# A decode step of attention and a gated unit: the output projection's weights in five loads instead of eight

## The chip, the cores and the metric

One core of a Trainium2 chip runs the whole kernel. The time is device microseconds (us) of one execution; lower is better. Before the change it is 684.75 us, the median of three runs (684.56 to 685.55).

## What is computed

One token of width 512 goes through a layer norm, then through attention with 32 heads over a cache of 8192 keys and values of width 128, all in float32, and through a gated unit. The two results are multiplied and added to the input.

```python
xn = _layernorm(x)
q = (xn @ wq).reshape(B, Sq, H, Dh).transpose(0, 2, 1, 3)
scores = jnp.einsum("bhqd,bhkd->bhqk", q, k_cache) * (Dh ** -0.5)
o = jnp.einsum("bhqk,bhkd->bhqd", softmax(scores), v_cache)
s = o.transpose(0, 2, 1, 3).reshape(B, Sq, H * Dh) @ wo
g = gated(xn, w_gate, w_up, w_down)
return x + s * g
```

Here `gated` stands for `_silu((sigmoid(xn @ w_gate) * (xn @ w_up)) @ w_down)`. The two caches hold 256 MB, `wq` and `wo` 8 MB each.

## The kernel before, in words

All large loads go through one queue, that of SyncE (SP), in an order written out by hand. `wq`, `w_gate` and `w_up` come first, then keys and values of two heads at a time (a pair; `NP` = 16 pairs), 8 MB of keys and 8 MB of values each, and last `wo`. Three buffers of 64 KB a partition, `slots`, hold them: keys alternate between slots 0 and 1, values use slot 2, and `wo` comes into slot 1 when the last keys there have been used (`summed[NP - 2]`). `load` (a DMA at line 168) and `load_values` (a DMA at line 227) issue them.

For each pair, VectorE multiplies the keys by the query and sums (`scores`, lines 415 and 416), ScalarE makes the powers (`powers_of`), and TensorE multiplies them with the values (`pair`): 32 products of 4 key positions each, in turn into four groups of 32 PSUM rows (the 32 columns of the array that write such a group are called a tile here). A float32 product runs as two passes in the profile. `taken` makes TensorE wait for a piece of values, and `halved` and `valued` tell SyncE that half or all of the slot may be loaded again. The values of the last two pairs come in pieces: `V_HALVES` is the halves of the 128 columns of blocks (`NB`), `V_THREE` cuts at 64 and 104.

All TensorE instructions are noted first (`Later`) and played at line 38, so line 38 is every TensorE instruction of the profile, and the pairs are a loop on that engine.

Behind the last pair the heads' results are turned and divided into `o_all` (`heads_out` and `place`, lines 423, 469 and 472). The projection by `wo` is 32 rows per partition (`WR`), of 2 KB each: row `r` of all partitions, 256 KB, times column `r` of `o_all`. Its loads end at the rows `W_ENDS`. Each row below `W_FOLD` = 28 is either TensorE's, one product of 512 columns into the tile that `W_PE` names, or VectorE's (`W_DVE`, lines 513 and 515), which adds into two sums, `part`, in turn. `landed` makes an engine wait at the first of its rows in a piece. Line 518 adds the two sums, `to_fold` (line 490) adds what TensorE has in `big[0]`, and `fold` sums over partitions, with four products of 128 columns. Rows 28 to 31 go directly into the result's form, `acc`, by four products of 128 columns each. In TensorE's order the fold stands behind row 30 and ahead of row 31. Lines 539 and 541 multiply by the gate and add the input, and line 565 stores.

Ahead of the `wo` rows TensorE makes two products into `po` whose result nobody reads; they wait for nothing ("idle products" here). SyncE waits for the last load but one of `wo` (`ld_o[-2]`, line 556) before it leaves the body.

Of the kernel before, what the change touches and what calls it, by code (L numbers as in the profile page):

```python
# [51 lines left out]
def kernel(  # L52
# [18 lines left out]
    NB = S // HP  # L71
    NP = H // 2
    NG = 4
# [14 lines left out]
    FC = FL // GP  # L88
    assert F <= 3 * QT and FL % GP == 0 and 2 * KT * F <= SLOT and (FP + FC) * D <= SLOT // 2

    W_ENDS, W_FOLD = (10, 18, 23, 26, 28, 30, 31, 32), 28
    W_PE = [(0, 0), (1, 0), (2, 0), (3, 0), (4, 0), (10, 1), (11, 1), (12, 1), (18, 2), (19, 2), (23, 2), (24, 3), (26, 2), (27, 3)]
    W_DVE = [r for r in range(W_FOLD) if r not in [r for r, _ in W_PE]]
    V_CUTS, K_CUTS = (NB // 2, NB * 13 // 16), {NP - 2: (NB * 3 // 4,), NP - 1: (NB // 2,)}

    N_SEMS = 38
    DVE, ACT, SP, POOL = nc.vector, nc.scalar, nc.sync, nc.gpsimd
    PE = Later(nc.tensor)
    pe_only = OrderedEngineSet([nc.tensor.engine])
# [2 lines left out]

    sems = [nc.alloc_semaphore(f"s_{i}") for i in range(N_SEMS)]
    s_out = nc.alloc_semaphore("s_out")
# [42 lines left out]
    def semaphore(name):  # L147
        return unused.pop(0)
# [25 lines left out]
    def wait(eng, *steps):  # L174
        for s in steps:
            if s is not None:
                eng.wait_ge(*s)


    turned, spread_m, valued, picked = (semaphore(f"s_{n}") for n in ("turned", "spread", "valued", "picked"))  # L180
    maxed, reduced, powers, copied = (semaphore(f"s_{n}") for n in ("maxed", "reduced", "powers", "copied"))
    added = semaphore("s_added")
    q_made, q_spread, q_free = (semaphore(f"s_{n}") for n in ("q_made", "q_spread", "q_free"))
    s_val = [semaphore(f"s_val{n}") for n in range(3)]
    halved = semaphore("s_halved")


# [14 lines left out]
    def rows_of(src, i):  # L202
        rows = src.rearrange("b h s d -> (b h s) d")[2 * i * S:2 * (i + 1) * S, :]
        return rows.rearrange("(p j) d -> p (j d)", p=P)
# [3 lines left out]
    def pieces(*ends):  # L208
        return [slice(a, b) for a, b in zip((0,) + ends, ends + (NB,))]

    FULL, V_HALVES, V_THREE = pieces(), pieces(V_CUTS[0]), pieces(*V_CUTS)

    def cols(j):
        return slice(j.start * Dh, j.stop * Dh)

    def load_keys(i, cut, *after):
        n = (i + 1) % 2
        wait(SP, *after)
        for j in cut:
            ld_k.setdefault(i, []).append((j, load(SP, f"k{n}_{j.start}", slots[n][:, cols(j)], rows_of(k_cache, i)[:, cols(j)])))  # L220

    def load_values(i, cut, *after):

        wait(SP, *after)
        for j in cut:
            sem = s_val[((0,) + V_CUTS).index(j.start)]
            SP.dma_start(slots[2][:, cols(j)], rows_of(v_cache, i)[:, cols(j)]).then_inc(sem, 16)  # L227

    load_keys(0, FULL)
# [10 lines left out]
    ld_xr = load(ACT, "xr", x_row[0:P:GP, :], xv.rearrange("(g c) -> g c", g=NG), c_xrow)  # L240
    ACT.nop().then_inc(q_free, NK)
    ACT.nop().then_inc(s_val[1], 16 * (NP - 2))
    ACT.nop().then_inc(s_val[2], 16 * (NP - 1))
    pool(POOL.memset(ones, 1.0))
    pool(POOL.memset(eps_t, EPS))
    pool(POOL.memset(zeros, 0.0))
# [35 lines left out]
    def taken(sem, n):  # L282
        PE.wait_ge(sem, n)
        PE.nop().then_inc(sem, -n)
# [72 lines left out]
    n = FL // NG  # L357
# [11 lines left out]
    wait(PE, act(ACT.copy(s_gate, big[0])))  # L369
    gated = column_sums(big[1], s_gate)  # L370
    load_values(0, FULL, gated)
    wait(ACT, gated)
    c_sig = act(ACT.activation(g_row, big[1][:, :GC], AF.Sigmoid))


    def pair(v):
        taken(maxed, 1)
        PE.matmul(pt[0:1, :], mx[:, 0:1], ident, start=True, stop=True).then_inc(turned, 1)
        taken(reduced, 1)
        PE.matmul(pm[:, :2], ones[:1, :], mx[:1, 1:3], start=True, stop=True).then_inc(spread_m, 1)  # L380
        taken(powers, 2)
        PE.matmul(pm[:GP, 2:], rs.to_broadcast([P, GP]), half, start=True, stop=True).then_inc(added, 1)

        for j in range(0, NB, HT):
            if j in (0,) + V_CUTS:
                if j == V_CUTS[0]:
                    ins.then_inc(halved, 1)
                taken(s_val[((0,) + V_CUTS).index(j)], 16)
            g = j // HT % NG
            ins = PE.matmul(po[g * GP:g * GP + 2 * HT, :], weights[:, j // HT, :], v[:, j * Dh:(j + HT) * Dh],  # L390
                            start=(j < HT * NG), stop=(j >= NB - HT * NG))
        ins.then_inc(valued, 1)
        taken(copied, 1)
        for b in range(HT):
            ins = PE.matmul(pn[:2, :], pick[:, b:2 * HT:HT], o1[:, b * Dh:(b + 1) * Dh],
                            start=(b == 0), stop=(b == HT - 1))
        ins.then_inc(picked, 1)

    before = PE.take()
    pair(slots[2])  # L400
    each = PE.take()

# [3 lines left out]
    def all_max(i):  # L406
        DVE.wait_ge(turned, i + 1)
        DVE.reduce_max(mx[:1, 1:3], pt[0:1, :].rearrange("o (e p) -> o e p", e=2), axis=AX.X).then_inc(reduced, 1)  # L408

    def scores(i):  # L410
        k = slots[(i + 1) % 2].rearrange("p (j d) -> p j d", d=Dh)
        for j, ld in ld_k[i]:
            wait(DVE, ld)
            n = j.stop - j.start
            wait(DVE, dve(DVE.tensor_mul(k[:, j, :], k[:, j, :], qb[:, i:i + 1, :].to_broadcast([P, n, Dh]))))  # L415
            summed[i] = dve(DVE.reduce_sum(sc[i % 2][:, j], k[:, j, :], axis=AX.X))  # L416
        wait(DVE, summed[i])
        DVE.reduce_max(mx[:, 0:1], sc[i % 2], axis=AX.X).then_inc(maxed, 1)

    def heads_out(i):  # L420
        DVE.wait_ge(picked, i + 1)
        o = o_t[:, 2 * WP * i:2 * WP * i + Dh].rearrange("r (e a) -> r a e", a=WP)
        turned_out[i] = dve(DVE.transpose(o, pn.rearrange("e (a r) -> e a r", r=WR)))  # L423


    def powers_of(i):
        ACT.wait_ge(spread_m, i + 1)
        wait(ACT, act(ACT.mul(nb, pm[:, :2], -SCALE)))  # L428
        for e, h in enumerate(HALF):
            ACT.activation(weights[h, :, e * HT:(e + 1) * HT], sc[i % 2][h].rearrange("p (g b) -> p g b", b=HT),  # L430
                           AF.Exp, bias=nb[h, e:e + 1], scale=SCALE, accum_out=rs[h]).then_inc(powers, 1)

    def parts(i):
        ACT.wait_ge(added, i + 1)
        t = act(ACT.copy(den[:GP, 2 * i:2 * i + 2], pm[:GP, 2:]))
        ACT.wait_ge(valued, i + 1)
        ACT.copy(o1, po).then_inc(copied, 1)  # L437
        return t

    for i in range(NP):  # L440
        if i > 0:
            all_max(i - 1)
        if i >= 2:
            load_keys(i, pieces(*K_CUTS.get(i, ())), summed[i - 2])
            if i < NP - 1:
                load_values(i - 1, FULL, (valued, i - 1))
        if i == NP - 1:
            for v, cut in ((i - 1, V_HALVES), (i, V_THREE)):
                load_values(v, cut[:1], (halved, v))
                load_values(v, cut[1:], (valued, v))  # L450
        scores(i)
        if i > 0:
            powers_of(i - 1)
            parts(i - 1)
            heads_out(i - 1)
        if i == 1:
            wait(DVE, c_sig)
            c_gate = dve(DVE.tensor_mul(g_row, g_row, big[1][:, :GC]))
# [43 lines left out]
    def landed(eng, r, rows):  # L502
        k = rows.index(r)
        wait(eng, piece[r] if k == 0 or piece[r] != piece[rows[k - 1]] else None)

    t_parts = [placed, None]
    for k, r in enumerate(W_DVE):
        n = k % 2
# [8 lines left out]
    wait(DVE, max(t_parts, key=lambda t: t[1]))  # L517
    t_part = dve(DVE.tensor_add(part[0], part[0], part[1]))

    for n in range(2):  # L520
        PE.matmul(po[:2 * HT, :], weights[:, 0, :], slots[2][:, n * QT:(n + 1) * QT], start=True, stop=True)
    wait(PE, placed)
    w_rows, w_tiles = zip(*W_PE)
    for k, (r, g) in enumerate(W_PE):
        landed(PE, r, w_rows)
# [76 lines left out]
```

## Time and profile before

| what | us |
|---|---|
| median of three runs | 684.75 |
| the profiled execution | 684.87 |
| its span in the profile | 683.5 |
| VectorE busy in it | 613.1 |
| TensorE busy in it (matmuls) | 222.8 |
| ScalarE busy in it | 44.5 |

The profile is one execution. Its span is from the first instruction to the last; the execution's own time is 1.37 longer. PE is TensorE's matmuls, PEld its weight loads, DVE VectorE, ACT ScalarE, SPq the queue of SyncE. Times in the rows further down are microseconds from the span's start. What is in brackets behind a row is how long the engine had been idle and what released it. "issue" there means that the profile shows nothing it waited for.

### The profile page before, as it was taken

The page shows a single profiled execution, that of the slowest core. Times are in us where ns is not written, and L with a number is a line of the kernel's source. Part 1 is how long each engine was busy: PE and PEld are TensorE (multiplying, and loading weights), DVE is VectorE, ACT ScalarE, POOL GpSimd, SP SyncE. Part 2 cuts the span into 40 slices and gives each one's busy share as a digit, 9 for nine tenths or more (in the row PEclk, how much of TensorE's full clock was granted, in tenths as well). Part 3 has the DMA queues.
Part 4 walks back from the last instruction along what each step waited for, and adds up shares of the span by engine and source line. Part 5 has one row for each costly group of instructions (what it writes and reads, how often), then busy time and mean ns, then how long its engine had stood idle before and what let it go on. Part 6 is the DMA issues. An engine that isn't in the chain of part 4 may idle for free. (4 is left out here: it accounts for less than half of the span.)

```text
span 683.5 us, 3414 instructions
## 1 busy us (share of the span) xinstructions
PE 222.8 (33%) x1386; PEld 63.6 (9%) x1386; DVE 613.1 (90%) x151; ACT 44.5 (7%) x142; POOL 2.6 (0%) x11
## 2 busy tenths in 40 slices
PE   0353024060513306050412406050422406060678
PEld 0120001010100101010100101010100101010111
DVE  3879999999999898998979899898979899999926
ACT  2130010000000100000000100000010100000010
POOL 0000000000000000000000000000000000000000
PEclk9996657575665757575665757575575757566789
DMA  9999999999999999999999999999999999999998
GB/s 386 429 436 468 433 430 430 430 430 430 430 430 430 430 430 430 430 430 449 456 445 430 430 430 430 430 430 430 430 430 430 445 449 410 476 399 430 430 430 338
DMA packets 7272, 293.68 MB, mean 430 GB/s; under 512 B 828, under 2 KB 840, under 8 KB 1512
## 3 DMA queue, kind: packets, MB, share of 16 engines
q1 hardware_dynamic: 7264, 293.67, 99.5%
q10 hardware_dynamic: 8, 0.00, 0.0%
HBM read 293.67 MB, written 0.00 MB: 430 GB/s over the span
## 5 line engine op out<-in xcount | busy, mean ns | idle before, releaser
L415 DVE TENSOR_TENSOR slot<-slot,q_all 128x16384 f32<-128x16384 f32 (+3 forms) x18 | 275.8, 15320 | 23.9 <-DMA slot<-in_A_k_cache_dram 23.9
L416 DVE TENSOR_REDUCE sc<-slot 128x128 f32<-128x16384 f32 (+3 forms) x18 | 275.8, 15324 | 0.6
L38 PE MATMUL psum<-slot,zeros 128*8 128x512 f32 x1028 | 150.2, 743 | 258.0 <-PEq L38 258.0
L38 PEld LDWEIGHTS psum<-slot,zeros 128*8 128x8 f32 x1028 | 30.9, 104 | 363.0 <-issue 363.0
L38 PE MATMUL psum<-ident,mx 128*1 128x128 f32 x32 | 8.8, 373 | 110.0 <-PEq L38 110.0
L437 ACT COPY o<-psum 128x512 f32<-128x512 f32 x16 | 9.4, 585 | 404.5 <-PE psum L38 404.5
L38 PE MATMUL psum<-slot,ones 128*128 (+3 forms) x36 | 15.9, 611 | 21.7 <-PEq L38 16.3
L290 DVE SCALAR_TENSOR_TENSOR slot<-slot,xn 128x1376 f32<-128x1376 f32 (+1 forms) x8 | 18.9, 2360 | 3.0 <-DMA slot<-in_A_wq_dram 2.7
L38 PE MATMUL psum<-o,pick 128*2 128x128 f32 x128 | 16.5, 272 | 12.8 <-PEq L38 12.8
L423 DVE STREAM_TRANSPOSE psum<-psum 32x128 f32<-32x128 f32 x16 | 4.9, 309 | 9.9 <-PE psum L38 9.9
L430 ACT ACTIVATE zeros<-sc,nb 64x128 f32<-64x128 f32 x32 | 12.8, 399 | 0.9
L38 PE MATMUL psum<-slot,o_all 128*1 128x128 f32 (+1 forms) x60 | 12.5, 421 | 0.9 <-DMA slot<-in_A_wo_dram 0.8
L428 ACT ACTIVATE nb<-psum 128x2 f32<-128x2 f32 x16 | 2.8, 172 | 152.5 <-PE psum L38 152.5
L38 PEld LDWEIGHTS psum<-o,pick 128*2 128x2 f32 x128 | 9.9, 84 | 29.7 <-issue 27.3
L38 PEld LDWEIGHTS psum<-ident,mx 128*1 128x1 f32 x32 | 1.8, 80 | 114.2 <-issue 114.2
L408 DVE TENSOR_REDUCE mx<-psum 1x2 f32<-1x128 f32 x16 | 4.5, 279 | 8.2 <-PE psum L38 8.2
L38 PE MATMUL psum<-zeros,rs 128*32 128x2 f32 x32 | 3.8, 187 | 23.5 <-PEq L38 23.5
L38 PE MATMUL psum<-mx,ones 1*128 1x2 f32 x32 | 8.4, 331 | 7.4 <-PEq L38 7.4
L38 PE MATMUL psum<-slot,o 128*1 128x512 f32 x26 | 5.7, 953 | 13.1 <-DMA slot<-in_B_w_down_dram 13.1
L515 DVE SCALAR_TENSOR_TENSOR q_all<-slot,o_all,q_all 128x512 f32<-128x512 f32 x12 | 8.1, 745 | 2.0 <-DMA slot<-in_A_wo_dram 2.0
L38 PEld LDWEIGHTS psum<-slot,ones 128*128 128x128 f32 (+1 forms) x36 | 6.2, 196 | 31.0 <-issue 23.2
L38 PEld LDWEIGHTS psum<-mx,ones 1*128 1x128 f32 x32 | 7.5, 291 | 14.4 <-issue 14.4
(54 smaller groups left out, 61.6 us busy)
## 6 DMA issues: line engine op xcount, KB each, us to landing
slot<-in_A_v_cache_dram SPq DMA_DIRECT2D x3, 4096.0 KB, 22.5
slot<-in_A_wq_dram SPq DMA_DIRECT2D x2, 4096.0 KB, 16.4
slot<-in_A_k_cache_dram SPq DMA_DIRECT2D x2, 4096.0 KB, 37.8
slot<-in_A_k_cache_dram SPq DMA_DIRECT2D x1, 6144.0 KB, 37.9
slot<-in_B_w_gate_dram SPq DMA_DIRECT2D x1, 2752.0 KB, 26.8
slot<-in_B_w_up_dram SPq DMA_DIRECT2D x1, 2752.0 KB, 32.8
slot<-in_B_w_down_dram SPq DMA_DIRECT2D x1, 2560.0 KB, 23.8
slot<-in_A_v_cache_dram SPq DMA_DIRECT2D x1, 2560.0 KB, 10.3
```

The lines of the kernel that those rows point to most:

```text
L38: ins = getattr(self.engine, name)(*args, **kwargs)
L290: return dve(DVE.scalar_tensor_tensor(y, w[:, k, cols], xn[:, k:k + 1], y, op0=ALU.mult, op1=ALU.add))
L408: DVE.reduce_max(mx[:1, 1:3], pt[0:1, :].rearrange("o (e p) -> o e p", e=2), axis=AX.X).then_inc(reduced, 1)
L415: wait(DVE, dve(DVE.tensor_mul(k[:, j, :], k[:, j, :], qb[:, i:i + 1, :].to_broadcast([P, n, Dh]))))
L416: summed[i] = dve(DVE.reduce_sum(sc[i % 2][:, j], k[:, j, :], axis=AX.X))
L423: turned_out[i] = dve(DVE.transpose(o, pn.rearrange("e (a r) -> e a r", r=WR)))
L428: wait(ACT, act(ACT.mul(nb, pm[:, :2], -SCALE)))
L430: ACT.activation(weights[h, :, e * HT:(e + 1) * HT], sc[i % 2][h].rearrange("p (g b) -> p g b", b=HT), AF.Exp, bias=nb[h, e:e + 1], scale= ...
L437: ACT.copy(o1, po).then_inc(copied, 1)
L515: ins = DVE.scalar_tensor_tensor(part[n], wo_t[:, r, :], col, part[n], op0=ALU.mult, op1=ALU.add)
```

## The change

`wo` comes in five loads instead of eight, of 16, 8, 4, 3 and 1 rows. The values of the last pair come in two halves, as those of the pair before do; the third semaphore for values, `s_val[2]`, goes. TensorE takes eighteen rows of `wo` below 28 instead of fourteen, with other tiles, VectorE ten instead of fourteen, and four idle products stand ahead of TensorE's rows instead of two.

```diff
-    W_ENDS, W_FOLD = (10, 18, 23, 26, 28, 30, 31, 32), 28
-    W_PE = [(0, 0), (1, 0), (2, 0), (3, 0), (4, 0), (10, 1), (11, 1), (12, 1), (18, 2), (19, 2), (23, 2), (24, 3), (26, 2), (27, 3)]
+    W_ENDS, W_FOLD = (16, 24, 28, 31, 32), 28
+    W_PE = [*zip(range(9), (0, 0, 0, 1, 0, 1, 0, 1, 0)), *zip(range(16, 21), (2, 3, 2, 3, 2)), *zip(range(24, W_FOLD), range(NG))]
     W_DVE = [r for r in range(W_FOLD) if r not in [r for r, _ in W_PE]]
-    V_CUTS, K_CUTS = (NB // 2, NB * 13 // 16), {NP - 2: (NB * 3 // 4,), NP - 1: (NB // 2,)}
+    V_CUT, K_CUTS = NB // 2, {NP - 2: (NB * 3 // 4,), NP - 1: (NB // 2,)}
...
-            if j in (0,) + V_CUTS:
-                if j == V_CUTS[0]:
+            if j % V_CUT == 0:
+                if j:
                     ins.then_inc(halved, 1)
-                taken(s_val[((0,) + V_CUTS).index(j)], 16)
+                taken(s_val[j // V_CUT], 16)
...
-            for v, cut in ((i - 1, V_HALVES), (i, V_THREE)):
-                load_values(v, cut[:1], (halved, v))
-                load_values(v, cut[1:], (valued, v))
+            for v in (i - 1, i):
+                load_values(v, V_HALVES[:1], (halved, v))
+                load_values(v, V_HALVES[1:], (valued, v))
...
-    for n in range(2):
+    for n in range(4):
         PE.matmul(po[:2 * HT, :], weights[:, 0, :], slots[2][:, n * QT:(n + 1) * QT], start=True, stop=True)
```

The order of instructions on TensorE behind the loop over pairs, before the change (`slot` with `zeros` are the idle products, `slot` with `o_all` the rows of `wo`, 512 columns or quarters of 128, `q_all` with `ones` the fold; s_30 to s_37 are the eight loads, s_1 is VectorE's steps):

```order
L38 MATMUL psum<-slot,zeros 8x512 x2
L38 MATMUL psum<-slot,o_all 1x512 [waits s_30,s_1]
L38 MATMUL psum<-slot,o_all 1x512 x4
L38 MATMUL psum<-slot,o_all 1x512 [waits s_31]
...
L38 MATMUL psum<-slot,o_all 1x512 [waits s_34]
L38 MATMUL psum<-slot,o_all 1x512
L38 MATMUL psum<-slot,o_all 1x128 [waits s_35]
L38 MATMUL psum<-slot,o_all 1x128 x7
L38 MATMUL psum<-slot,o_all 1x128 [waits s_36]
L38 MATMUL psum<-slot,o_all 1x128 x3
L38 MATMUL psum<-q_all,ones 1x128 [waits s_1]
```

The same place after the change (s_29 to s_33 are the five loads):

```order
L38 MATMUL psum<-slot,zeros 8x512 x4
L38 MATMUL psum<-slot,o_all 1x512 [waits s_29,s_1]
L38 MATMUL psum<-slot,o_all 1x512 x8
L38 MATMUL psum<-slot,o_all 1x512 [waits s_30]
L38 MATMUL psum<-slot,o_all 1x512 x4
L38 MATMUL psum<-slot,o_all 1x512 [waits s_31]
L38 MATMUL psum<-slot,o_all 1x512 x3
L38 MATMUL psum<-slot,o_all 1x128 [waits s_32]
L38 MATMUL psum<-slot,o_all 1x128 x11
L38 MATMUL psum<-q_all,ones 1x128 [waits s_1]
```

TensorE waits five times for `wo` instead of eight, and the twelve quarter products of rows 28 to 30 now stand behind one wait, where rows 28 and 29 had one and row 30 its own.

SyncE's queue at the end of the values and at `wo`, as the difference (- before, + after; 128x8192 is 4 MB):

```order
-L227 DMA slot2<-in_A_v_cache_dram 128x5120 [waits s_6]
-L227 DMA slot2<-in_A_v_cache_dram 128x3072
-L168 DMA slot1<-in_A_wo_dram 128x5120 [waits s_1]
+L227 DMA slot2<-in_A_v_cache_dram 128x8192 [waits s_6]
+L168 DMA slot1<-in_A_wo_dram 128x8192 [waits s_1]
 L168 DMA slot1<-in_A_wo_dram 128x4096
-L168 DMA slot1<-in_A_wo_dram 128x2560
+L168 DMA slot1<-in_A_wo_dram 128x2048
 L168 DMA slot1<-in_A_wo_dram 128x1536
-L168 DMA slot1<-in_A_wo_dram 128x1024 x2
-L168 DMA slot1<-in_A_wo_dram 128x512 x2
+L168 DMA slot1<-in_A_wo_dram 128x512
```

The last values are one load where they were two, and `wo` five where it was eight; what SyncE waits for ahead of them stays.

## Rows read from the trace of the kernel before

**Rows 1.** The page, GB/s in 40 equal slices of the span.
```profile
GB/s 386 429 436 468 433 430 430 430 430 430 430 430 430 430 430 430 430 430 449 456 445 430 430 430 430 430 430 430 430 430 430 445 449 410 476 399 430 430 430 338
```
**Rows 2.** The chain that ended last, its end: start us, us, what.
```profile
647.16 0.33 SPq L227
...
647.53 0.43 SPq L227
...
651.53 29.21 DMA slot<-in_A_wo_dram
...
680.79 0.44 PE psum L38 x8
...
681.25 0.30 DVE g_row L539
```
**Rows 3.** DMA issues: size of each, median us from issue to landing.
```profile
slot<-in_A_wo_dram SPq DMA_DIRECT2D x1, 2560.0 KB, 19.1
...
slot<-in_A_v_cache_dram SPq DMA_DIRECT2D x1, 1536.0 KB, 13.6
...
slot<-in_A_wo_dram SPq DMA_DIRECT2D x2, 256.0 KB, 29.2
```
**Rows 4.** Timeline of the tail: start us, us, engine, line, operation, [idle before <-releaser].
```profile
654.43 9.71 PE L38 MATMUL psum<-slot,zeros 128*8 128x512 f32 x64
...
663.11 0.10 PEld L38 LDWEIGHTS psum<-slot,zeros 128*8 128x8 f32 x4 [0.33 <-issue]
...
665.82 1.88 PE L38 MATMUL psum<-slot,zeros 128*8 128x512 f32 x4
...
667.17 0.88 DVE L513 TENSOR_SCALAR q_all<-slot,o_all 128x512 f32<-128x512 f32 x2 [0.37 <-DMA slot<-in_A_wo_dram]
...
667.96 2.07 DVE L515 SCALAR_TENSOR_TENSOR q_all<-slot,o_all,q_all 128x512 f32<-128x512 f32 x3
...
672.04 0.09 PEld L38 LDWEIGHTS psum<-slot,o_all 128*1 128x1 f32 x2 [0.99 <-DMA slot<-in_A_wo_dram]
...
675.14 0.09 PEld L38 LDWEIGHTS psum<-slot,o_all 128*1 128x1 f32 x2 [1.30 <-DMA slot<-in_A_wo_dram]
...
676.97 0.09 PEld L38 LDWEIGHTS psum<-slot,o_all 128*1 128x1 f32 x4 [0.89 <-DMA slot<-in_A_wo_dram]
...
678.18 0.09 PEld L38 LDWEIGHTS psum<-slot,o_all 128*1 128x1 f32 x4 [1.12 <-DMA slot<-in_A_wo_dram]
...
679.25 0.69 DVE L490 TENSOR_TENSOR q_all<-q_all,psum 128x512 f32<-128x512 f32 x1 [0.46 <-PE psum L38]
679.42 0.33 PEld L38 LDWEIGHTS psum<-slot,o_all 128*1 128x1 f32 x16 [1.15 <-DMA slot<-in_A_wo_dram]
...
680.12 0.11 PEld L38 LDWEIGHTS psum<-slot,o_all 128*1 128x1 f32 x8 [0.37 <-DMA slot<-in_A_wo_dram]
...
680.34 0.40 PE L38 MATMUL psum<-q_all,ones 128*1 128x128 f32 x8
680.78 0.10 PEld L38 LDWEIGHTS psum<-slot,o_all 128*1 128x1 f32 x8 [0.34 <-DMA slot<-in_A_wo_dram]
```
**Rows 5.** Timeline of TensorE's matmuls alone, in three narrow windows.
```profile
667.53 4.46 PE L38 MATMUL psum<-slot,o_all 128*1 128x512 f32 x10
...
676.97 0.60 PE L38 MATMUL psum<-slot,o_all 128*1 128x512 f32 x2
...
677.40 0.60 PE L38 MATMUL psum<-slot,o_all 128*1 128x512 f32 x2
```
**Rows 6.** Stretches: window, its us, PE busy (x), granted clock, DMA share, GB/s.
```profile
638.00:640.00 2.00, 0.00 (x0) 1.00 0.80 344
640.00:642.00 2.00, 0.21 (x4) 1.00 1.03 442
642.00:644.00 2.00, 2.00 (x16) 0.69 1.21 524
...
658.00:660.00 2.00, 2.00 (x16) 0.54 0.99 424
```

More of the change, by code (lines that the diff above doesn't have):

```diff
@@ L89 @@
     assert F <= 3 * QT and FL % GP == 0 and 2 * KT * F <= SLOT and (FP + FC) * D <= SLOT // 2
-    W_ENDS, W_FOLD = (10, 18, 23, 26, 28, 30, 31, 32), 28
-    W_PE = [(0, 0), (1, 0), (2, 0), (3, 0), (4, 0), (10, 1), (11, 1), (12, 1), (18, 2), (19, 2), (23, 2), (24, 3), (26, 2), (27, 3)]
+    W_ENDS, W_FOLD = (16, 24, 28, 31, 32), 28
+    W_PE = [*zip(range(9), (0, 0, 0, 1, 0, 1, 0, 1, 0)), *zip(range(16, 21), (2, 3, 2, 3, 2)), *zip(range(24, W_FOLD), range(NG))]
     W_DVE = [r for r in range(W_FOLD) if r not in [r for r, _ in W_PE]]
-    V_CUTS, K_CUTS = (NB // 2, NB * 13 // 16), {NP - 2: (NB * 3 // 4,), NP - 1: (NB // 2,)}
-    N_SEMS = 38
+    V_CUT, K_CUTS = NB // 2, {NP - 2: (NB * 3 // 4,), NP - 1: (NB // 2,)}
+    N_SEMS = 34
     DVE, ACT, SP, POOL = nc.vector, nc.scalar, nc.sync, nc.gpsimd
@@ L183 @@
     q_made, q_spread, q_free = (semaphore(f"s_{n}") for n in ("q_made", "q_spread", "q_free"))
-    s_val = [semaphore(f"s_val{n}") for n in range(3)]
+    s_val = [semaphore(f"s_val{n}") for n in range(2)]
     halved = semaphore("s_halved")
@@ L209, in pieces @@
         return [slice(a, b) for a, b in zip((0,) + ends, ends + (NB,))]
-    FULL, V_HALVES, V_THREE = pieces(), pieces(V_CUTS[0]), pieces(*V_CUTS)
+    FULL, V_HALVES = pieces(), pieces(V_CUT)
     def cols(j):
@@ L225, in load_values @@
         for j in cut:
-            sem = s_val[((0,) + V_CUTS).index(j.start)]
+            sem = s_val[j.start // V_CUT]
             SP.dma_start(slots[2][:, cols(j)], rows_of(v_cache, i)[:, cols(j)]).then_inc(sem, 16)
@@ L242 @@
     ACT.nop().then_inc(s_val[1], 16 * (NP - 2))
-    ACT.nop().then_inc(s_val[2], 16 * (NP - 1))
     pool(POOL.memset(ones, 1.0))
```

## The prediction

> **What bounds the kernel now.** I read the page first: its DMA rate is 430 GB/s in most slices and 399 to 476 in all but the first and the last [rows 1], so the kernel is one long stream of bytes from memory. The change alters no byte of it. What it can move is how smoothly the last 12 MB of the stream come in, and what is left to do once they are there.
>
> The chain that ended last says the same of the tail [rows 2]: SyncE issues the last values and then `wo` (from 647.16 on), 29.21 us pass waiting for `wo` to land, and behind that stand only 0.44 us of TensorE, two short VectorE operations and the store. The DMA issues [rows 3] give the start of the `wo` stretch: the last piece of values, issued at 647.53, takes 13.6 us, so it is there at 661.13; the first piece of `wo`, issued behind it at 648.0, takes 19.1 us, so 667.1.
>
> The timeline of the tail [rows 4] is the view that carries the sum. In it the reader sees when each piece of `wo` released an engine: 667.17 (to row 10), 672.04 (18), 675.14 (23), 676.97 (26), 678.18 (28), 679.42 (30), 680.12 (31), 680.78 (32). Row 31's eight passes take 0.40, as the fold's at 680.34 do, so TensorE ends at 681.19, and VectorE follows at 681.25 [rows 2]. A narrow look at TensorE [rows 5] gives the price of a pass, and the table of stretches [rows 6] its clock.
>
> **The sum, part by part.**
>
> *The stream.* One row of `wo` is 256 KB. Between the releases above a row costs 0.609 us (10 to 18), 0.62 (18 to 23), 0.61 (23 to 26), 0.605 (26 to 28), 0.62 (28 to 30), then 0.70 and 0.66 for the two pieces of one row [rows 4]. Pieces of one row cost some 0.05 to 0.09 more; the others hardly differ. The new pieces, priced by the nearest size: 16 rows x 0.607 = 9.71, 8 x 0.609 = 4.87, 4 x 0.605 = 2.42, 3 x 0.61 = 1.83, the last 0.68. From 661.13 they release their users at 670.85, 675.72, 678.13, 679.96 and 680.64. The last is 0.14 earlier than 680.78. The values' second half in one piece instead of two saves one more boundary; what a boundary costs there no row isolates. Bounds: nothing, and 0.09, the dearest boundary of the `wo` loads; I take 0.05, nearer the middle since those pieces are large. The queue is never empty meanwhile: the pieces of `wo` are issued 19.1 to 29.2 us before they land [rows 3], so four issues fewer on SyncE, 0.47 us each with the gap [rows 2], are worth nothing by themselves. SyncE's wait before it leaves is now for the three-row piece, which lands no later than the row it waited for before.
>
> *The values of the last pair.* TensorE ends them at 654.43 + 9.71 = 664.14 [rows 4]. The second half is sixteen products, thirty-two passes, four side by side with a step of 0.10 + 0.33 = 0.43: 8 x 0.43 and 0.16 for the last to drain, so it begins at 660.5, before all of the values are there. After the change it waits for 661.1 and ends at 664.7. So the values are 0.56 late, and with them the copy, the picking, and VectorE's placing of `o_all`. Its first `wo` operation at 667.17 now waits for the first piece at 670.85 anyway; 3 us of cover. Without that cover the 0.56 would be paid in full.
>
> *Four idle products instead of two.* Two took four passes of 0.43 from 665.82 [rows 4]. Four take eight, 3.43, and from 666.38 end at 669.8, still 1.05 before the first row of `wo` is there. They cost nothing as long as the clock is at its upper level.
>
> *Eighteen rows on TensorE.* Ten passes in one tile took 4.46: nine steps of 0.43 and 0.59 for the last [rows 5]. A row is two passes. Rows 23 and 24, of tiles 2 and 3, ran side by side: two passes start at 676.97, two at 677.40 [rows 5]. So what counts is the longest queue of one tile. First piece: rows 0, 1, 2, 4, 6, 8 in tile 0 are twelve passes, 5.15 us, 670.85 to 676.00; rows 3, 5, 7 hide in tile 1. Second piece, at 675.72: rows 16, 18, 20 in tile 2 are six passes, 2.57, until 678.3. Third piece, at 678.13: one row for each tile, two passes; tile 2 is free last, at 678.3, so 679.15, and 0.16 to drain: 679.3.
>
> The Trainium skill, page "TensorE: Matmul & The Clock Gate", Part 3, says under "What overlaps and what doesn't" that matmuls are in program order in start and end, with no reordering; by that rule rows 24 to 27 take five turns instead of two and the kernel would end near 686.0. The trace speaks against it here: in program order the second pass of row 23 would start before or with the first of row 24, and [rows 5] show both first passes starting together and both second ones 0.43 later.
>
> *VectorE.* Seven rows of the first piece: 0.88 for the first two and five at 2.07 / 3 = 0.69 give 675.2; three of the second piece from 675.72 end at 677.8; adding the halves, 0.69 as at 679.25 [rows 4], 678.5. So adding TensorE's sum starts when TensorE is through, 679.3, and ends at 680.05 instead of 679.94. It is needed only after rows 28 to 30.
>
> *The end.* Passes over a quarter row step by 0.11 in fours: eight take 0.40, of which 0.29 is the last one's [rows 4]. Rows 28, 29 and 30 now come together at 679.96, six steps, 0.65, until 680.61; the fold of the sum, 0.22, until 680.83; row 31, there at 680.64, starts behind it and ends 0.40 later, at 681.23. Before, row 30 alone and the fold were through in the gap ahead of row 31. So of the 0.14 that the stream gives, the larger last-but-one piece takes back all: 681.23 against 681.19, +0.04; with 0.05 from the values, -0.01. The bounds: stream gains nothing, 681.19 + 0.18 = +0.18; stream gains everything that its best row rate allows, 32 x 0.605 = 19.36 and the values' 0.09, so -0.29 - 0.09 for the landing, of which the tail keeps 0.18: -0.2.
>
> The profiled execution took 684.87 against a median of 684.75. The sum gives 684.86 for it, so **684.7** for the median. This is no change: a measurement of this kernel can tell some 0.2%, 1.4 us, from none.
>
> **The rivals.**
>
> *Each load costs the stream a fixed price.* There are four loads fewer (three of `wo`, one of values). At the dearest boundary in the rows, 0.09, that is 0.36, and 684.4, if the tail keeps none of it back; to be told apart it would have to be 0.34 for each load. Against it: one-row pieces land 0.66 to 0.70 apart where their bytes take 0.61 [rows 4]. The Trainium skill, page "DMA: Bandwidth & Descriptors", section on the anatomy of one DMA, fits a DMA as about 2.0 us and its bytes at 436 GB/s; four of these would be 8 us and give some 676.8. The trace disagrees, by the same 0.66.
>
> *TensorE's clock falls ahead of the first piece.* This one ends slower. TensorE is idle from 669.8 to 670.85 in the forecast. If the clock fell to the lower level there, as it did between 642 and 644, after a stretch from 638 with 0.21 us of work until 642 [rows 6], passes would take 0.86. It rose again at about 659.8, 5.4 us after the values began [rows 4, 6]; so long at half pace loses 2.7 us. Rows 0 to 8 end at 678.7, rows 16 to 20 at 680.4, row 26 at 681.45, the sum is added at 682.2, and after fold and row 31 it is 682.85: +1.65, **686.4**. For it: twice as many rows come at once, and the idle stretch stands right ahead of them. Against it: 638 to 640 passed with no TensorE work at all and a granted clock of 1.00, the upper of its two levels, 2.4 GHz [rows 6]. It decides if TensorE idles ahead of the first piece as long as it did from 638 to the end of that stretch, so if the idle products end near 667.
>
> *TensorE takes the passes strictly in turn.* Then rows 24 to 27 end near 680.4, the sum is added at 681.2, the fold and row 31 take five turns each: 682.4, +1.2, 686.0, just inside what cannot be told. [Rows 5] speak against it.
>
> *The change doesn't reach the path at all*, since the stream sets the end whatever is cut: 684.75 exactly. It cannot be told from my forecast by time, only by the release times.
>
> **How the numbers follow.** Forecast, with the bounds of its costs and with the rival that nothing reaches the path: 0.80. A fixed price for each load: 0.08, of which 0.02 is large enough to be seen. Clock falls: 0.05. Strict turns: 0.04, half of it over the bound. Unforeseen: 0.03, mostly within. That gives faster 0.03, same 0.90, slower 0.07. The range takes the sum's bounds, -0.2 and +0.2, the 0.36 of the first rival, and the spread of the runs shown, 0.2 below their median and 0.8 above it: 684.1 to 685.6. It leaves out the clock and the strict turns, less than 1 in 10.
>
> **What would show it.** First `wo` release at 670.8, then 675.7, 678.1, 680.0, 680.6; TensorE's values ending near 664.7; a granted clock of 1.00 from 660 to the end; VectorE's addition of TensorE's sum near 679.35; fold and row 31 back to back with no wait between. Wrong would be a stretch after 666 with a lower clock, passes of rows 24 to 27 one by one, a last release earlier than 680.4 or later than 680.8, or a fold that waits for VectorE.

## The result, and the profile after

The changed kernel takes 686.64 us, the median of nine runs (685.76 to 688.11), against 684.84 for the kernel before, measured beside it (684.48 to 685.55). The ratio is 1.0026, 95% interval 1.0017 to 1.0035: slower by 1.8 us. The forecast was 684.7, no change, with a range up to 685.6.

The profiled execution took 687.69, the second longest of the nine, so its trace shows more of the loss than the median has; its span is 686.3. The end of its chain (start us, us, what), against [rows 2]:

```profile
642.82 6.41 PE psum L38 x32
...
649.25 0.33 SPq L227
...
651.10 31.60 DMA slot<-in_A_wo_dram
...
682.74 1.32 PE psum L38 x40
```

The wait for `wo`, here for its piece of three rows, is 31.60 us where the wait for the last row was 29.21. SyncE issues the last values at 649.25 instead of 647.16, because TensorE's second half of the values of the pair before started at 642.82 and took 6.41 us. In the kernel before, the chain has it like this:

```profile
641.79 5.35 PE psum L38 x32
...
647.16 0.33 SPq L227
```

The timeline of the tail, against [rows 4]:

```profile
663.98 3.62 PE L38 MATMUL psum<-slot,zeros 128*8 128x512 f32 x32 [3.31 <-PEq L38]
...
669.26 3.60 PE L38 MATMUL psum<-slot,zeros 128*8 128x512 f32 x8
...
673.55 0.88 DVE L512 TENSOR_SCALAR q_all<-slot,o_all 128x512 f32<-128x512 f32 x2 [3.31 <-DMA slot<-in_A_wo_dram]
...
678.38 0.09 PEld L38 LDWEIGHTS psum<-slot,o_all 128*1 128x1 f32 x4 [0.35 <-DMA slot<-in_A_wo_dram]
...
680.84 0.20 PEld L38 LDWEIGHTS psum<-slot,o_all 128*1 128x1 f32 x8 [0.66 <-DMA slot<-in_A_wo_dram]
682.03 0.69 DVE L489 TENSOR_TENSOR q_all<-q_all,psum 128x512 f32<-128x512 f32 x1 [0.87 <-PE psum L38]
682.74 0.54 PEld L38 LDWEIGHTS psum<-slot,o_all 128*1 128x1 f32 x24 [1.70 <-DMA slot<-in_A_wo_dram]
...
683.61 0.40 PE L38 MATMUL psum<-slot,o_all 128*1 128x128 f32 x8
```

The releases are at 673.55, 678.38, 680.84 and 682.74, each 2.7 to 2.8 behind the forecast's 670.85, 675.72, 678.13 and 679.96; their distances are as forecast. So the tail works as worked out, and all of it starts late. TensorE's clock in the tail is not the reason: it is at its upper level from 660 us on (window, us, PE busy, granted clock, DMA share, GB/s):

```profile
660.00:664.00 4.00, 0.69 (x12) 1.00 0.95 410
664.00:668.00 4.00, 3.60 (x32) 1.00 0.93 401
668.00:672.00 4.00, 3.61 (x15) 1.00 1.02 438
672.00:676.00 4.00, 3.19 (x12) 1.00 0.95 408
676.00:680.00 4.00, 4.00 (x18) 1.00 0.98 413
680.00:684.00 4.00, 3.23 (x52) 1.00 0.26 102
```

The stream itself shows why. In the same columns, the last microseconds one by one; first the kernel before, where the last row is there at 680.78:

```profile
679.00:680.00 1.00, 0.78 (x18) 1.00 1.04 401
680.00:681.00 1.00, 0.88 (x28) 1.00 0.23 86
```

and the changed kernel:

```profile
679.00:680.00 1.00, 1.00 (x6) 1.00 0.97 401
680.00:681.00 1.00, 1.00 (x8) 1.00 0.71 285
681.00:682.00 1.00, 0.98 (x9) 1.00 0.26 100
682.00:683.00 1.00, 0.26 (x12) 1.00 0.06 23
```

Before, all 16 DMA engines stop together. After, most are through at 681, and from 682 on 0.06 of them, one of the sixteen, still works. A load is there when its last engine is done. The page's third part has a queue that the kernel before doesn't have; cut to 106 to 109 us (packets, MB, share of 16 engines):

```profile
q1 hardware_dynamic: 16, 1.05, 81.6%
q8 instruction: 1, 0.02, 1.9%
```

It is one packet of 16 KB of program, a fetch of instructions. TensorE doesn't wait for it: its passes go on at 0.43 us each from 105.90 to 108.91. Up to 100 us the sixteen DMA engines finished each load of the changed kernel within 0.4 us of each other; from the next load on, which lands at 120.70, one of them is 1.3 us later than the rest. It makes up 0.2 us in the next 500 (the engines are 1.63 us apart at 120 us and 1.42 at 642) and no more: every engine is busy to the end.

### The profile page after: what moved, and what is told of

Same layout as the page of the kernel before. It is cut to its first block, busy times and chain, and to the rows that moved or that the text cites. A ratio compares the mean times of both kernels' runs of the same rounds, so it can differ in the third digit from the quotient of the medians.

```text
span 686.3 us, 3411 instructions
## 1 busy us (share of the span) xinstructions
PE 224.4 (33%) x1398; PEld 65.1 (9%) x1398; DVE 611.6 (89%) x147; ACT 44.5 (6%) x142; POOL 2.6 (0%) x11
## 5 line engine op out<-in xcount | busy, mean ns | idle before, releaser
L38 PE MATMUL psum<-slot,zeros 128*8 128x512 f32 x1032 | 153.3, 747 | 255.1 <-PEq L38 255.1
L38 PE MATMUL psum<-slot,ones 128*128 (+3 forms) x36 | 17.9, 672 | 21.6 <-PEq L38 16.2
L38 PE MATMUL psum<-slot,o_all 128*1 128x512 f32 (+1 forms) x68 | 9.6, 441 | 1.6 <-DMA slot<-in_A_wo_dram 1.6
L310 ACT COPY q_all<-psum 64x256 f32<-64x256 f32 x16 | 5.9, 366 | 20.8 <-PE psum L38 20.3
## 6 DMA issues: line engine op xcount, KB each, us to landing
slot<-in_A_v_cache_dram SPq DMA_DIRECT2D x4, 4096.0 KB, 19.1
```

The source lines that it names most:

```text
L38: ins = getattr(self.engine, name)(*args, **kwargs)
L310: ins = ACT.copy(qb[h, 2 * t:2 * t + 2, :], q[h, :, e, :])
```

## The experiments

Theory CODE: the change makes TensorE's program longer (107 products where it had 101, each idle product and each row being one), this brings the fetch, and the fetch sets one DMA engine back. Rival LOADS: the larger loads are served less evenly. Numbers of the profiled executions, read from the trace: when SyncE issued the last values, when the first engine was through with all before them, how far the sixteen were apart there and at the end of `wo`, and when the last row of `wo` had landed. Each ratio is against runs of the kernel before on the same chip in the same session, whose medians were 684.99 for e1 to e4 and 684.75 for e5 to e8; the 684.84 in the first row is that of the session with the changed kernel.

| kernel | products | fetch at | issue | first engine through | apart, then | last landing | median (ratio, interval) |
|---|---|---|---|---|---|---|---|
| before | 101 | none | 647.16 | 651.07 | 0.27, 0.33 | 680.74 | 684.84 |
| the change | 107 | 107 | 649.25 | 650.94 | 1.54, 2.63 | 683.32 | 686.64 (1.0026, 1.0017 to 1.0035) |
| e9, the change again | 107 | 107 | 648.15 | 650.78 | 1.58, 2.03 | 681.98 | one run, 686.34 (685.12 before, one run) |
| e1, before, more code | 107 | 107 | 648.05 | 651.15 | 1.10, 1.32 | 681.84 | 686.41 (1.0022, 1.0012 to 1.0032) |
| e2, the change, less code | 101 | none | 647.84 | 650.45 | 0.54, 0.54 | 680.17 | 684.86 (0.9999, 0.9990 to 1.0008) |
| e3, before, two halves | 101 | none | 648.28 | 651.23 | 0.39, 0.38 | 680.90 | 684.89 (0.9998, 0.9989 to 1.0007) |
| e4, the change, two idle | 105 | 681.4 | 646.72 | 650.34 | 0.56, 0.55 | 680.06 | 686.00 (1.0015, 1.0006 to 1.0024) |
| e5, before, late values | 101 | none | 648.87 | 650.95 | 0.30, 0.92 | 681.38 | 685.53 (1.0013, 1.0004 to 1.0023) |
| e6, e2 with late values | 101 | none | 649.35 | 650.59 | 0.32, 0.50 | 680.89 | 685.30 (1.0010, 1.0000 to 1.0020) |
| e7, sixteen rows, two idle | 103 | 685.4 | 648.41 | 650.89 | 0.43, 0.46 | 680.51 | 687.57 (1.0039, 1.0024 to 1.0053) |
| e8, sixteen rows, none idle | 101 | 685.6 | 646.68 | 650.83 | 0.68, 0.72 | 680.72 | 685.18 (1.0001, 0.9992 to 1.0011) |

The record has the span of every run, not only of the profiled ones. Its median is 685.3 us with the change and 685.1 in e1, the two kernels with a fetch at 107 us; it is 683.5 and 683.4 for the kernel before beside e1 to e4 and e5 to e8, and 683.5, 683.4, 683.6, 683.4 and 683.7 in e2, e3, e4, e7 and e8. So the longer span comes with the early fetch in the runs without a trace too. e4 and e7 compute everything and have the change's loads; they show that its absence in e2 is not due to what e2 leaves out.

**Code added to the kernel before (e1).**

```diff
     for n in range(2):
         PE.matmul(po[:2 * HT, :], weights[:, 0, :], slots[2][:, n * QT:(n + 1) * QT], start=True, stop=True)
+    for n in range(6):
+        PE.matmul(po[:2 * HT, :1], weights[:, 0, :], slots[2][:, n:n + 1], start=True, stop=True)
```

> The kernel before, with six more idle products on TensorE, one column wide each, behind its two. Loads, rows and their engines stay as before. Theory CODE (the longer TensorE program of the change makes one code fetch of 16 KB during the pairs, on one of the 16 DMA engines, which then stays 1.3 us behind): the fetch is there, the last-but-one values are about 1 us late, the last row of wo lands at 682 or later, and the time is 685.8 to 687. Theory LOADS (the larger loads of the last values and of wo are served less evenly): no fetch, last release at 680.8, 684.8, within 0.3 of before.

1.4 us slower, with every load as before. The fetch is there (106 to 109 us again), and the stream ends in the changed kernel's way:

```profile
q8 instruction: 1, 0.02, 1.9%
```

```profile
680.00:681.00 1.00, 0.78 (x18) 1.00 0.46 176
681.00:682.00 1.00, 0.91 (x30) 1.00 0.05 20
```

LOADS falls as the cause of this part: six products of one column, twelve passes that start 0.025 us after one another and take 0.3 us in all, cost 1.4 us. A little of that is the second part below: the engines are 1.10 apart ahead of the last values and 1.32 behind them.

**Code taken out of the change (e2).**

```diff
-    for c in range(FP + FC):
+    for c in range(FP + FC - 6):
...
-                        start=(c < NG), stop=(c + NG >= FP + FC))
+                        start=(c < NG), stop=(c + NG >= FP + FC - 6))
```

> The changed kernel with seven products by w_down instead of thirteen, so that part of the gate is left out; TensorE has as many products in its program as before the change. The end of the kernel is the change's. Theory CODE: no fetch, the 16 engines stay within 0.5 us of each other, the last release of wo is at 680.6 and the time 684.7, within 0.3 of before. Theory LOADS: the packets of the last values' second half are stretched as in the changed kernel, last release above 681.5, 685.7 or more.

This kernel leaves out six of the thirteen products by `w_down`, so its gate is not the whole one; everything else is the change's. The whole loss is gone, with the change's loads, rows and idle products all in place: 684.86. No instruction queue is left in the page, and the tail is the one that was forecast:

```profile
670.39 0.88 DVE L512 TENSOR_SCALAR q_all<-slot,o_all 128x512 f32<-128x512 f32 x2 [3.30 <-DMA slot<-in_A_wo_dram]
...
675.27 0.09 PEld L38 LDWEIGHTS psum<-slot,o_all 128*1 128x1 f32 x4 [0.39 <-DMA slot<-in_A_wo_dram]
...
677.73 0.21 PEld L38 LDWEIGHTS psum<-slot,o_all 128*1 128x1 f32 x8 [0.65 <-DMA slot<-in_A_wo_dram]
678.92 0.69 DVE L489 TENSOR_TENSOR q_all<-q_all,psum 128x512 f32<-128x512 f32 x1 [0.87 <-PE psum L38]
679.58 0.54 PEld L38 LDWEIGHTS psum<-slot,o_all 128*1 128x1 f32 x24 [1.65 <-DMA slot<-in_A_wo_dram]
...
680.23 0.40 PE L38 MATMUL psum<-q_all,ones 128*1 128x128 f32 x8
680.45 0.40 PE L38 MATMUL psum<-slot,o_all 128*1 128x128 f32 x8
```

**The halves alone (e3).** `V_THREE` becomes the halves in the kernel before, and the third semaphore for values goes with it, nothing else.

> The kernel before with the last pair's values in two halves, nothing else. TensorE's program gets a wait shorter. Theory CODE: no fetch, values done near 664.7 instead of 664.1, hidden only in part since the first piece of wo comes at 667.2: TensorE's rows 0.5 later, which the waits for later pieces take up; 684.8, within 0.4 of before. Theory LOADS: the single 4 MB load of the second half is stretched, last release 0.5 to 1.2 later, 685.3 to 686.

684.89, no fetch, and the engines as close together behind the last values as ahead of them (0.39, 0.38). The last 4 MB of values as one load do no harm.

**Two idle products in the change (e4).**

```diff
-    for n in range(4):
+    for n in range(2):
```

> The changed kernel with two idle products instead of four, so TensorE's program is two products shorter than the change's and four longer than before. Theory CODE: either the program still makes the fetch, and the time is the change's, 686 to 687, or it is short enough, and the time is 684.7. Theory LOADS: 686 to 687 without a fetch. In all cases TensorE idles some 2.7 us ahead of the first piece; if the granted clock then falls, the passes of rows 0 to 8 take 0.86 and the end comes up to 1.6 us later still.

The time is that of the first branch of the expectation, 686.0 with a fetch, but not in its way: the stream ends at 680.06, the earliest of all, and the span is 683.1. The fetch has moved. From 681 to 683 us, behind the last row of `wo`:

```profile
q8 instruction: 1, 0.02, 4.1%
```

The profiled execution took 685.59, so 2.5 us lie outside its span, where the kernel before has 1.4. In all ten runs it is 2.3 to 2.5; the kernel before has 1.3 to 1.7 in 55 of the 58 runs beside the experiments (2.6 to 2.9 in the other three). The loss, 1.0 us by the medians, is now at the end of the program. How a fetch there makes the end later no trace shows.

**The second part: late issue (e5, e6).** In the trace of the changed kernel the sixteen are 1.54 apart ahead of the last values and 2.63 apart behind them. SyncE issues these values 2.1 us later than before, only 1.7 ahead of the moment when the first engines run out. Two delays add up there. The late engine lets the values of the pair before land 1.04 us later; and TensorE takes 6.41 us for them instead of 5.35, with a granted clock of 0.50 from 643 to 647 us, where the kernel before has 0.50 to 645 and 0.71 from there to 647. The second delay is not the fetch's: e2 has it without a fetch,

```profile
641.42 6.41 PE psum L38 x32
```

and the second trace of the change (e9) has the late landing without it:

```profile
642.78 5.36 PE psum L38 x32
```

To try a late issue without the fetch, the issue waits for a later step:

```diff
-                load_values(v, cut[1:], (valued, v))
+                load_values(v, cut[1:], (valued if v < i else picked, v))
```

> The kernel before, where SyncE issues the last pair's last two pieces of values only after TensorE has also picked the heads of the pair before (some 1.8 us later, near 649.0; the first DMA engine is through with what it has at 651.07). No code fetch. Theory LATE ISSUE (a load that is issued less than some 2 us before the first engine runs out starts with stretched packets, which is the second part of the change's loss): a small stretch, engines' spread up from 0.3 to between 0.5 and 1.5, time 685.0 to 686.0. Rival (the issue's time is harmless as long as an engine still has work; the fetch alone explains all): spread stays at 0.3, 684.9, within 0.3 of before.

> The changed kernel with six products by w_down left out (as in the run with less code, so part of the gate is missing), and the last values issued only after the picking: near 649.6, 0.9 before the first engine runs out at 650.4. No code fetch. LATE ISSUE: most engines stretch their first packets, spread from 0.55 to 1 or more, last release of wo at 681 to 682 instead of 680.2, time 685.5 to 686.5. Rival: 680.2 and 684.9.

e5 is 0.8 us slower than the kernel before beside it (685.53 against 684.75) and e6 0.55 (685.30); e5's interval leaves out no change, e6's touches it, and there is no fetch in either. e5 came out as its theory said. e6 came out between its two branches (0.50 apart, 680.89, 685.30). In e5 one engine ends 0.92 behind the first and the next 0.53, where all were within 0.30 ahead of the late load. In e6 all do: its first engine needs 10.3 us for the 4 MB (650.59 to 660.88) where in e2 it needs 9.7. The stretch is in the first packets of the late load: twelve of those of 32 KB take 1.7 to 2.0 us in e6, and some up to 2.56 in the changed kernel, instead of 1.21. The rival, that a queue which isn't empty is enough, falls: an issue 2.1 us ahead of the first engine's end was late in e5 (its last landing is 681.38 against 680.74 before), one 1.2 us ahead in e6 (680.89 against 680.17 in e2).

The other traces bear this out, though they show no sharp bound. Each of the eleven has two loads of values that wait for TensorE: the second half of the pair before the last, and the second half of the last pair (its first piece, where there are two). From the end of the load ahead to the end of such a load the sixteen engines need, in the mean, 9.68 us for 4 MB and 6.08 for 2.5 MB when nothing is lost. Issued 3.2 us or more ahead of the first engine's end, eight loads lost 0.02 us at most. Issued 2.4 to 3.1 us ahead, seven of ten lost at most 0.06 us; the two of e9 lost 0.17 and 0.20, and one of e1 lost 0.11. Issued 2.1 us ahead or less, all four lost, 0.17 to 0.87. What happens in the DMA hardware no run shows.

**Sixteen rows, with two idle products and with none (e7, e8).** Rows 8 and 20 go to VectorE.

```diff
-    W_PE = [*zip(range(9), (0, 0, 0, 1, 0, 1, 0, 1, 0)), *zip(range(16, 21), (2, 3, 2, 3, 2)), *zip(range(24, W_FOLD), range(NG))]
+    W_PE = [*zip(range(8), (0, 0, 0, 1, 0, 1, 0, 1)), *zip(range(16, 20), (2, 3, 2, 3)), *zip(range(24, W_FOLD), range(NG))]
```

> The changed kernel with two idle products and sixteen rows on TensorE (rows 8 and 20 go to VectorE), 103 products in TensorE's program where before has 101, the change 107, and the run with two idle products 105. Everything is computed. Theory CODE: short enough, no fetch, 684.8; or the program's end is still fetched late, as with 105, and the time is 686.0. VectorE's rows end near 678.3 plus 0.69, before TensorE's, so the tail doesn't change: release of the last row at 680.2 if there is no fetch.

> The same sixteen rows without any idle product, 101 products as before the change. Everything is computed. Theory CODE: no fetch, engines within 0.6 of each other. TensorE then idles about 4 us ahead of the first piece of wo, at 666.3 to 670.4. If the granted clock falls there, passes of the first rows take 0.86 and the end comes 0.6 to 1.6 later than without (685.4 to 686.4); if it holds, 684.8.

e7 (103 products) takes 687.57, the slowest of all and above both branches of its expectation, though its last row lands at 680.51 and its span is 683.5: 4.3 us of its 687.83 lie outside the span, and the trace has a packet of 16 KB of program there, at 685.4. In all five runs 4.0 to 4.4 us lie outside. e8 (101 products) is at 1.0001 (0.9992 to 1.0011), no change; its engines are 0.7 us apart, a little over the 0.6 that was expected. Its profiled run, 686.73, the longest of its ten, has such a packet at 685.6 too, and 3.0 us outside the span; its other nine runs have 1.3 to 1.7. In e8 the granted clock did fall ahead of the first piece, behind 4.2 us without TensorE work:

```profile
668.00:672.00 4.00, 0.96 (x2) 0.55 0.93 397
672.00:676.00 4.00, 4.00 (x14) 0.60 0.95 403
```

It cost nothing, where the expectation had 0.6 to 1.6: with sixteen rows TensorE was through with the first two pieces at 677.67 and then waited 0.56 us for the third.

**The change once more (e9).**

> The changed kernel once more, for a second trace. Theory CODE with LATE ISSUE: the code fetch is at 107 us again, one engine is 1.1 to 1.5 us behind from then on; the last values are issued 1 to 2 us later than 647.2, and how much is lost there varies: last release of wo between 681.5 and 683.5, time 685.7 to 688.1. Theory CHANCE (the fetch in the first trace was a single event): no fetch, 684.8.

The fetch comes at the same place, so it is no chance. The issue at 648.15 is 2.6 us ahead of 650.78, and less is lost there than in the first trace: the engines go from 1.58 to 2.03 apart, 0.45 us where that one has 1.09. That may be the scatter of the changed kernel's runs, 685.8 to 688.1; two traces don't settle it.

No version beat the kernel before beyond its interval: e2, e3 and e8 are at 0.9998 to 1.0001.

## Why the prediction was wrong

**The step that failed** is the costing of the added products: "They cost nothing as long as the clock is at its upper level", and for the rows, that only the longest queue of one tile counts. Both count TensorE's time. The instructions themselves also have a price, which I put at nothing: six products more bring a fetch of 16 KB through one of the sixteen DMA engines, on a kernel whose bound is just those engines. e1 shows its size without the rest of the change, 1.4 us, and e2 that the rest of the change without it is worth nothing, as forecast. Only the 0.03 for what was unforeseen covered it, "mostly within" the range. The prediction also took 1.4 us as what a measurement can just tell from none; the interval here is 0.6 us to either side.

**The second failed step** is "The queue is never empty meanwhile". To the letter it held, for the last values were still issued 1.7 us ahead; but that is not enough. It was read from the median time between issue and landing, 19.1 to 29.2 us, of the `wo` loads; the load that mattered is the one ahead of them, the values, issued only 3.9 us before the first engine ran out in the kernel before. e5 and e6 show that this distance has a price at 2.1 us and less. How much of the change's 1.8 us is due to it stays open: the intervals of e1 and of the change overlap.

What held, by e2, whose stream as a whole ran 0.4 us earlier than the forecast's from the first piece of `wo` on:

- The distances of the releases: 4.9, 2.5 and 1.85 in e2 (DVE at 670.39, then 675.27, 677.73, 679.58), forecast 4.87, 2.41 and 1.83.
- TensorE's passes side by side: rows 24 to 27 are released at 677.73 and summed from 678.92, 1.2 later, as the two turns forecast. In strict turns it would have been 2.3.
- The fold and row 31 stand back to back behind rows 28 to 30 (680.23 and 680.45, no wait between), so the larger last-but-one piece takes back what the stream gives.
- The clock held at 1.00 in the changed kernel from 660 on, so that rival was not what made it slower, although it too forecast a slower kernel.
- The price of a load. The interval of e2's ratio leaves room for the 0.36 us of the rival with a fixed price, so the time doesn't decide. The traces do: from the first engine's end with all before the last values to its end with `wo` it is 29.35 us before, 29.29 with the halves alone (e3), and 29.16 to 29.17 in e2, e4, e7 and e8. Four loads fewer give 0.18, half of what that rival has; the sum had 0.14 and 0.05. The 2.0 us that the prediction takes from the Trainium skill, page "DMA: Bandwidth & Descriptors", section "Anatomy of one DMA", stand there for DMAs that GpSimd issues; these loads are SyncE's, and the traces show 0.05 us for one of them.

The Trainium skill, page "Runtime: NRT & Kernel Launch", section "Instruction fetch mechanics", says that a sequencer fetches its program in blocks of 16 KB over a DMA queue of its own and that the cost of crossing such a boundary is mostly hidden. The trace agrees on the block, 0.02 MB in one packet on q8, and TensorE itself doesn't wait for it; but the cost is not hidden, since the DMA engine that brings the block is late with its data: 1.4 us in e1.

## What to carry to other kernels

In a kernel whose DMA engines never rest, look at the page's list of queues for an instruction queue, in the kernel before and after: here a few instructions more on TensorE brought a fetch, one DMA engine fell behind, and every later load waited for that one. Test an unexplained loss by adding as many empty instructions to the old kernel and by taking as many from the new one. And a queue's slack is read at the load that is issued last before the first engine runs out, not at the ones behind it.

## What the runs showed of the hardware that was not expected

- Where the fetch comes goes with the program's length: with 107 products at 107 us (three traces of three), with 105 at 681.4, with 103 behind the span, with 101 none within it (in one of six profiles of 101, that of e8, behind the span). The losses beside it are 1.4 to 1.8 us, 1.0 and 2.7. Why it comes early in the longest program is open.
- One packet of 0.93 us sets its DMA engine back by 1.0 to 1.3 us, and 570 us of further loads make good 0.2 to 0.4 us of that at most.
- Loads issued 2.1 us or less before the first DMA engine ran out were served late, though the queue was not empty: all four lost 0.17 to 0.87 us in the mean of the engines, and eight issued 3.2 us ahead or more lost 0.02 at most.
- A late landing is passed on: 1.04 us at the last-but-one values became 2.1 us at the issue of the last in the first trace of the change, where TensorE also had the lower clock for longer, and 1.0 us in the second (e9), where it had not.
